# Attention with chosen key chunks, then a squared-ReLU FFN: two heads' scores in 64-row halves, and a mask by DMA

## The chip, the cores and the metric

The kernel runs on one core of a Trainium2 chip. The metric is device time in microseconds, from one launch to the next result; smaller is better. A core has five engines that run side by side, each through its own list of instructions in order: TensorE (PE in the profile; its weight loads are PEld), VectorE (DVE), ScalarE (ACT), GpSimd (POOL) and SyncE (SP). DMA transfers are issued by SP and POOL here and run beside all of them.

## The reference

Four sequences of 768 positions, eight heads of 64, in float32. Keys are cut into 24 chunks of 32. For every query an upper bound of its score with each chunk is made from the chunk's smallest and largest key values; the six best causal chunks are kept, and causal softmax attention runs over those chunks alone. Its output goes through an FFN of 512 to 2048 to 512 with a squared ReLU.

```python
k_min = np.min(k_chunks, axis=3)
k_max = np.max(k_chunks, axis=3)
ub = np.sum(np.maximum(q[:, :, :, None, :] * k_min[:, :, None, :, :],
                       q[:, :, :, None, :] * k_max[:, :, None, :, :]), axis=-1)
ub = np.where(causal, ub, -1000000000.0)
top_chunks = np.argsort(ub, axis=-1)[..., -top_k:]
scores = scale * np.matmul(q, k.transpose(0, 1, 3, 2))
sel = (j_chunk == top_chunks[..., None]).any(axis=-2)
mask = sel & (pos[:, None] >= pos[None, :])
...
return (h * h @ w_out).astype(np.float32)     # h = relu(x @ w_in)
```

## The kernel before

Everything is in bfloat16 with float32 sums. A **tile** is 128 positions, so a sequence has six. The first tile of each sequence sees at most four chunks, so nothing has to be chosen there: `first_attention` (line 556) does plain causal attention for it, and the four first tiles together are one FFN of 512 rows. The other five tiles (640 rows) of each sequence are handled by **pairs** of heads: p = 0 to 15, four pairs a sequence, so pairs 8 to 15 are the last two sequences.

For each pair `stage_a` (line 622) makes the selection. Keys and queries are turned so that the head dimension lies on partitions (by PE for sequences 0 and 1, by DMA transposes on SP for 2 and 3). DVE takes minima and maxima of 32 keys at a time (`kr`, line 690, two passes over 768 columns), splits the queries into a positive and a negative part (`qp`, `qm`, line 706), PE multiplies them (`ub`, lines 656 and 658), DVE adds the causal mask of chunks (line 715), takes the eight best of each row (MAX8, line 664), and compares with the sixth (`selb`, line 720). The comparison is turned (`sT`), and copied into the operands of the scores.

Those operands have 88 rows for one head: 64 of the head and 24 for the chunks. The extra rows of the keys hold -32768 in their own chunk, those of the queries hold 1 for every chunk that was not chosen, so that one matmul gives scores with the unchosen chunks pushed far down. `kqs` and `qss` are the two operands, in four sets, and each head's rows are copied there (`copy`, lines 289 and 291).

`stage_b` (line 759) takes a pair's two heads one after the other. Each head has 20 tiles of scores (key tile by query tile) in five **banks** of four tiles or 512 columns (the list BANKS). For each bank: scores on PE (line 775), exp on ACT (line 797), the diagonal tiles made causal by POOL (line 755) or DVE (line 752), then the product with the values on PE (line 786). `normalise` (lines 604 and 606) divides by the sum.

`ffn` (line 816) turns x (`turn`: by PE for the first tiles and sequences 0 and 3, by DMA for 1 and 2), multiplies with w_in (`up`, line 859), takes ReLU on ACT or DVE (lines 866, 868), squares on DVE (line 877), and multiplies with w_out (`down`, line 890). FFN work of one sequence lies between the attention of the next on PE.

The order of all this is made when the program is built: each operation is given to a `Plan` (line 78) with its engines, costs and a due time, and `order` (line 116) places, again and again, the operation that is due first among those that can start soonest. So each engine's list is fixed in the built program. Where PE would have nothing to do in the first 30 us, `write` (line 203) fills in dummy matmuls (`keep_warm`, line 532, tile `wt`). POOL issues all loads of inputs and weights in a given order with eight outstanding at most; SP issues four first loads, all DMA transposes and the outputs.

Of the kernel before, what the change touches and what calls it, by code (L numbers as in the profile page):

```python
# [9 lines left out]
F32 = mybir.dt.float32  # L10
# [67 lines left out]
class Plan:  # L78
# [13 lines left out]
    NEVER = 1e9  # L92

    def __init__(self, slots, keep_warm, wait):
        self.wait = wait
# [20 lines left out]
    def order(self):  # L116
# [13 lines left out]
        while ready:  # L130
            found = []
            for op in ready:
                if op.packets and not op.turns and op is not self.loads[len(landed)]:
                    continue
                at = 0.0
                new = {}
                for t in op.tiles:
                    if not t.held:
                        new[t.tag] = new.get(t.tag, 0) + 1
                for tag, n in new.items():  # L140
                    at = max(at, sorted(slots[tag])[n - 1][0]
                             if n <= len(slots[tag]) else self.NEVER)
                if at == self.NEVER:
                    continue
                if op.packets and not op.turns and len(landed) >= 8:
                    at = max(at, landed[-8].end)
                for engine, cost in op.where.items():
                    st = max(at, free[engine])
                    for n in op.needs:
                        same = n.engine == engine and not n.packets  # L150
                        lag = (0.0 if engine == "PE" else self.BUSY) if same                             else self.HAND_OVER[n.engine]
                        st = max(st, n.end + lag)
                    for t in op.tiles:
                        if t.psum:
                            for e, end in t.last.items():
                                if e != engine and "PE" not in (e, engine):
                                    st = max(st, end + self.HAND_OVER[e])
                    found.append((st, op, engine, cost))
            assert found, "nothing can start"
            first = min(found, key=lambda f: (f[0], f[1].number))  # L160
            st, op, engine, cost = min(
                (f for f in found if f[2] == first[2] and f[0] <= first[0] + self.wait),
                key=lambda f: (round(f[1].due, 6), f[0], f[1].number))
            ready.remove(op)
# [22 lines left out]
            for n in waiting.get(op, ()):  # L187
                count[n] -= 1
                if not count[n]:
                    ready.append(n)  # L190
            done.append(op)
        assert len(done) == len(self.ops), "operations left"
# [10 lines left out]
    def write(self):  # L203
        idle = 0.0
        for op in self.order():
            if op.engine == "PE":
                free, *bank = self.spare(op.start - 1e-6)
                room = op.start - max(idle, free + self.EARLY)
                if idle and op.start < self.FILL and room >= self.LEAST:
                    self.keep_warm(bank, int((room - self.SPARED) / 0.1092))  # L210
                idle = op.end
            for t in op.tiles:
                if t.tile is None:
                    t.tile = t.make(t.slot)
            op.fn(op.engine)


@with_exitstack
def kernel(
# [51 lines left out]
    psav = ctx.enter_context(tc.tile_pool(name="psav", bufs=1, space=PSUM))  # L271
    psf = ctx.enter_context(tc.tile_pool(name="psf", bufs=1, space=PSUM))

    plan = Plan({"tp": 1, "ps": 3, "av": 2, "ff": 2, "e": 6, "h2": NFI + 6, "ht": 3,
                 "ob": 3, "kq": 6, "nt": 6,
                 "vn": B - 1, "x": 2, "xT": 2,
                 "kr": 2, "qp": 2, "qm": 2, "ubm": 2, "m8": 2, "rc": 2}, lambda *a: keep_warm(*a), P["wait"])
# [709 lines left out]
```

## Time and profile before

| | before |
|---|---|
| median of 3 runs | 263.65 us (263.57 to 263.76) |
| span of the profiled execution | 262.1 us |
| PE busy | 254.6 us, 2435 matmuls |
| DVE busy | 192.2 us |
| ACT busy | 180.2 us |
| POOL busy | 109.4 us |
| DMA | 26.12 MB, 103733 packets |

The profiled execution is known by its span, from its first to its last instruction; its own time with what lies around the span was not taken apart, so the span is set against the median of the runs. In the rows shown further on, a group has a line of the kernel, an engine, an operation, the tiles written and read, a count, then busy us and the mean ns of one, and last the idle time of the engine just before. In rows by time the first two numbers are the start and the length in us. PE busy is counted up to modelled ends, and matmuls overlap, so starts say more than lengths.

### The profile page before, as it was taken

Reading aid. Unit: us, or ns where it says so; the run is one execution under the profiler, and the core shown is the slowest. Engines: PE = TensorE matmul, PEld = TensorE weight load, DVE = VectorE, ACT = ScalarE, POOL = GpSimd, SP = SyncE. Lnnn points to the kernel's source line nnn. Section 1 sums busy time; section 2 is a strip of 40 time slices with the busy share of each in tenths; the row PEclk is TensorE's granted clock in tenths of the full one; section 3 lists DMA queues with packets and bytes.
Section 4 is the critical chain, followed back from the end, with each engine's and each line's share of the span. In section 5 each row is a group of like instructions: output and inputs, shape, how many; then the busy total and the mean of one; then the engine's idle time right before and its main releaser. Section 6 shows DMA issues by size and latency. Waiting matters only on the chain.

```text
span 262.1 us, 6645 instructions
## 1 busy us (share of the span) xinstructions
PE 254.6 (97%) x2435; PEld 168.2 (64%) x2457; DVE 192.2 (73%) x677; ACT 180.2 (69%) x369; POOL 109.4 (42%) x196
## 2 busy tenths in 40 slices
PE   8899999999999999999999999999999999999995
PEld 4678765756687666656786656657767576565443
DVE  5399999968999999999999995886778531254000
ACT  1589798856599888986799847768889351377112
POOL 8997999978416729993121011411103000000000
PEclk9999999999999999999999999999999999999999
DMA  8999999999982999999571011163000011200222
GB/s 134 168 176 187 143 186 166 185 155 195 185 119 46 115 129 175 145 153 134 102 147 57 0 56 43 59 120 94 0 3 0 3 40 40 84 1 0 83 80 80
DMA packets 103733, 26.12 MB, mean 100 GB/s; under 512 B 96332, under 2 KB 100708, under 8 KB 103700
## 3 DMA queue, kind: packets, MB, share of 16 engines
q0 software_dynamic: 75168, 13.33, 65.9%
q1 hardware_dynamic: 28532, 12.36, 22.2%
q8 instruction: 19, 0.31, 0.5%
q14 instruction: 14, 0.11, 0.1%
HBM read 27.26 MB, written 6.29 MB: 128 GB/s over the span
## 4 chain that ended last, share of the span: by engine, by line
PE 89%; ACT 3%; DMA 3%; DVE 2%; issue 1%; SPq 1%; POOL 0%; ACTq 0%; POOLq 0%
PE py L890 31%; PE ph L859 31%; PE ps L775 13%; PE av L786 7%; DMA raw<-in_q_dram 3%; PE wt L537 1%; PE xt L294 1%; ACT qsc L289 1%; ACT ht L866 1%; PE kT L294 1%; SPq L406 1%; PE ub L658 1%; DVE kr L690 1%; PE ub L656 1%; PE qT L294 1%
## 5 line engine op out<-in xcount | busy, mean ns | idle before, releaser
L859 PE MATMUL ph<-xT,w_in_sb 128*128 128x256 bf16 (+2 forms) x592 | 98.0, 304 | 0.5 <-ACT ht L866 0.2
L797 ACT ACTIVATE e<-ps 128x512 bf16<-128x512 f32 x160 | 86.6, 604 | 10.8 <-PE ps L775 6.3
L890 PE MATMUL py<-w_out_sb,h 128*128 128x512 bf16 (+2 forms) x378 | 88.2, 370 | 1.2
L755 POOL TENSOR_SCALAR_AFFINE_SELECT e<-e 128x128 bf16<-128x128 bf16 (+1 forms) x102 | 34.8, 353 | 88.4 <-ACT e L797 79.7
L859 PEld LDWEIGHTS <-w_in_sb 128*128 128x128 bf16 x592 | 55.4, 97 | 24.5 <-issue 1.8
L866 ACT ACTIVATE ht<-ph 128x256 bf16<-128x256 f32 (+2 forms) x122 | 54.9, 455 | 17.2 <-PE ph L859 13.5
L877 DVE TENSOR_TENSOR h<-ht 128x256 bf16<-128x256 bf16 (+2 forms) x148 | 47.4, 330 | 19.9 <-ACT ht L866 13.1
L890 PEld LDWEIGHTS <-h 128*128 128x128 bf16 x400 | 36.5, 98 | 33.1
L775 PE MATMUL ps<-qsc,kqc 88*128 88x128 bf16 (+1 forms) x320 | 54.4, 272 | 0.0
L289 ACT COPY ob<-py 128x512 f32<-128x512 f32 (+2 forms) x22 | 12.5, 568 | 37.3 <-PE py L890 37.2
L786 PEld LDWEIGHTS <-e 128*128 128x128 bf16 x640 | 31.8, 97 | 7.9 <-POOL e L755 0.9
L775 PEld LDWEIGHTS <-kqc 88*128 88x128 bf16 x320 | 27.0, 98 | 11.9 <-issue 0.2
L786 PE MATMUL av<-vn,e 128*128 128x65 bf16 x480 | 32.0, 193 | 0.2 <-POOL e L755 0.2
L606 DVE TENSOR_TENSOR x<-av,rc 128x320 bf16<-128x320 f32 (+1 forms) x40 | 18.6, 470 | 0.3
L690 DVE TENSOR_REDUCE kr<-kT 128x24 bf16<-128x768 bf16 x16 | 14.8, 948 | 1.4 <-PE kT L294 1.4
L664 DVE MAX8 m<-ubm 128x8 f32<-128x24 f32 x160 | 15.6, 169 | 0.0
L690 DVE TENSOR_REDUCE kr<-kt 128x24 bf16<-128x768 bf16 x16 | 14.9, 944 | 0.0
L868 DVE TENSOR_SCALAR ht<-ph 128x256 bf16<-128x256 f32 (+2 forms) x26 | 12.2, 471 | 3.7 <-PE ph L859 3.6
L289 ACT COPY qsc<-sT 24x384 bf16<-24x384 bf16 (+1 forms) x32 | 14.1, 440 | 0.8
L786 PE MATMUL av<-v,e 128*128 128x65 bf16 x160 | 14.0, 193 | 0.0
L454 POOL DMA_DIRECT2D vn<-in_v_dram x15 | 13.3, 901 | 0.5 <-issue 0.5
L537 PE MATMUL wt<-warm 128*128 128x256 bf16 x73 | 11.5, 301 | 1.1 <-DVE warm L358 1.1
(84 smaller groups left out, 251.3 us busy)
## 6 DMA issues: line engine op xcount, KB each, us to landing
out_dram<-ob SPq DMA_DIRECT2D x23, 256.0 KB, 2.3
w_in_sb<-in_moe_w_in_dram POOLq DMA_DIRECT2D x4, 512.0 KB, 7.6
w_out_sb<-in_moe_w_out_dram POOLq DMA_DIRECT2D x4, 512.0 KB, 8.3
vn<-in_v_dram POOLq DMA_DIRECT2D x15, 128.0 KB, 5.7
nt<-in_k_dram POOLq DMA_DIRECT2D x10, 128.0 KB, 5.4
nt<-in_q_dram POOLq DMA_DIRECT2D x10, 128.0 KB, 5.7
kn<-in_k_dram POOLq DMA_DIRECT2D x8, 80.0 KB, 6.7
qn<-in_q_dram POOLq DMA_DIRECT2D x8, 80.0 KB, 6.7
```

Of the source, the lines that this page charges most:

```text
L289: nc.scalar.copy(dst, src)
L606: return plan.op({"DVE": 0.06 + 0.00108 * D * n}, due, lambda _: nc.vector.tensor_mul(x(), av[:, :, 0:D], rc[:, 0:n].unsqueeze(2).to_broad ...
L664: nc.vector.max(out=m8[:, i, hh], in_=ubm[:, i, hh])
L690: nc.vector.tensor_reduce(kr[:, mm].rearrange("d (t c) -> d t c", c=128 // CH) if b >= BY_DMA else kr[:, mm], part(kT).rearrange("d t (c j ...
L755: nc.gpsimd.affine_select(out=e, in_=e, compare_op=ALU.is_ge, fill=0.0, base=0, channel_multiplier=-1, pattern=[[0, n], [1, 128]])
L775: nc.tensor.matmul(ps[:, 128 * c:128 * (c + nt)], lhsT=kqs[:, s, hh, 128 * j:128 * (j + 1)], rhs=qss[:, s, hh, 128 * (t0 - 1):128 * (t0 - ...
L786: nc.tensor.matmul(av[:, t - 1], lhsT=e[:, 128 * c:128 * (c + 1)], rhs=value_tile(b, h, j), start=(i == 0 and c == 0), stop=(i == len(BANK ...
L797: nc.scalar.activation(e.tile, ps.tile, ACT.Exp, scale=scale), [sc], [ps, e])
L859: nc.tensor.matmul(ph.tile, lhsT=w_in_sb[:, ki, 128 * f:128 * (f + 1)], rhs=xT[:, c0 // 128:c1 // 128, ki], start=(ki == 0), stop=(ki == N ...
L866: nc.scalar.activation(ht.tile, ph.tile, ACT.Relu)
L877: {"DVE": 0.067 + w / 1920}, at[0] + P["h2"], lambda _: nc.vector.tensor_mul(h2[f][:, c0:c1], ht.tile, ht.tile), [op], [ht, h2[f]])))
L890: nc.tensor.matmul(py.tile, lhsT=h2[f][:, 128 * t:128 * (t + 1)], rhs=w_out_sb[:, f, c0:c1], start=(f == 0), stop=(f == NFI - 1))
```

## The change

It has five parts, which stand in one diff.

1. **Pairs 8 to 15.** Their score operands are no longer the copies of 88 rows. The two heads' keys and queries are read where the DMA transposes put them, one head in partitions 0 to 63, the other in 64 to 127, and the matmuls of the two heads stand next to each other (`stage_b_rows`). They come in three groups a pair: four banks, four, two. The first key tile comes from a new tile `k1t`, which `first_transposes` fills.
2. **The mask.** Without the extra rows the choice is applied after exp. The turned selection of a pair is written to DRAM four times (`rowm`), then read back by six transfers that repeat each chunk's row over its 32 keys (`keep`, two buffers of 20 tiles x 2 heads). POOL makes the diagonal tiles of the mask causal, and DVE multiplies each bank's e with it: 80 multiplies, in the place of selects on the diagonals alone.
3. **Passes of DVE.** Minima and maxima of sequences 2 and 3 by a tree of halving passes over two pairs at once; the causal mask of chunks is added to the diagonal chunks alone, MAX8 reads only the chunks that can be seen, and copies and negative parts may go to ACT. Squares may go to ACT.
4. **Smaller ones.** The last sequence's x is turned by DMA; the first attention of sequences 2 and 3 has its diagonal cut after exp rather than by matmuls ahead of the scores (`preset`); the score operands have two sets, not four; `early` holds the first queries and later the first x.
5. **The order.** `Plan.order` takes each engine's list from ORDER, written out by number; costs and due times no longer decide it. Dummy matmuls stand only behind the first ten, which now come just ahead of pair 0's scores.

Counts in the two built programs:

| | before | after |
|---|---|---|
| PE: matmuls in all | 2459 | 2377 |
| PE: dummies (`wt`) | 73 | 15 |
| PE: transposes of x | 56 | 36 |
| PE: presets of 512 columns | 8 | 4 |
| DVE: mask multiplies | 0 | 80 |
| DVE: squares / ReLUs | 148 / 26 | 89 / 58 |
| ACT: squares / ReLUs | 0 / 122 | 59 / 90 |
| POOL: selects on e / on the mask | 102 / 0 | 46 / 40 |
| SP: plain transfers of the mask | 0 | 80 |
| SP: DMA transposes of x | 10 | 15 |

```diff
@@ Plan.order
-        ready = [op for op in self.ops if not count[op]]
+        at = {e: 0 for e in self.given}
+        while len(done) < len(self.ops):
             found = []
-            for op in ready:
+            for engine, line in self.given.items():
+                op = self.ops[line[at[engine]]]
...
+ORDER = {e: [int(i) for i in text.split()] for e, text in {
+    "PE": """
+        129 145 127 125 130 141 277 143 170 282 132 146 138 172 288 174 148 157 185 155 341
...
@@ kernel
-    VW = 80
+    VW = 72
     NSET = 4
+    KSET = 2
+    RP = 8
+    ROWS = RP // NP
+    COPIES = 4
...
-        s = plan.op({"PE": 0.44}, due - 5, preset, [made["ahead"], made["ident"], q0.op if b > 1 else None], ps)
+        s = None
+        if b < 2:
+            s = plan.op({"PE": 0.44}, due - 5, preset, [made["ahead"], made["ident"]], ps)
...
+            if b > 1:
+                e = plan.op({"DVE": 0.33, "POOL": 0.62}, due + 0.4, lambda en, hh=hh:
+                            causal(en, es[hh].tile, NP), [e, made["tri"]], [es[hh]])
...
+    def spread(p, t, sT, rowm, due):
+        m = keep[p]
+        held_back = kept_before[-1:]
+        out = [plan.op({"SP": 0.5}, due + 0.1 * i, lambda _, i=i: nc.sync.dma_start(
+            out=rowm.tile[:, i].rearrange("c t hh q -> c t (hh q)"),
+            in_=sT.tile[0:NC * NS].rearrange("x hh q -> x (hh q)")),
+            [t], [sT, rowm], packets=160, turns=True, late=0.7)
+            for i in range(COPIES)]
+        kept = {}
+        for j in range(NT):
+            n = NT - max(1, j)
+            kept[j] = plan.op({"SP": 0.5}, due + 1 + 0.1 * j, lambda _, j=j, n=n: nc.sync.dma_start(
+                out=m[:, ROW[j]:ROW[j] + n].rearrange("k t hh q -> k (t hh q)"),
+                in_=rowm.tile[4 * j:4 * j + 4, :, max(1, j) - 1:NS].rearrange(
+                    "a r t hh q -> (a r) (t hh q)").unsqueeze(1).to_broadcast(
+                        [4 * COPIES, CH // COPIES, 256 * n])),
+                out + held_back, [rowm, m], packets=200 * n, turns=True, late=0.7)
...
+    HELD = [(0, 1), (2, 3), (4,)]
...
+            def scores(_, banks=banks, pss_=pss_):
+                for i in banks:
+                    c = 0
+                    for j in range(NT):
...
+                        for hh in range(2):
+                            rows = slice(D * hh, D * hh + D)
+                            nc.tensor.matmul(
+                                pss_[i, hh][:, 128 * c:128 * (c + len(ts))],
+                                lhsT=keys(rows, j),
+                                rhs=queries(rows, ts[0], ts[-1] + 1),
+                                start=True, stop=True)
...
+                    mu = plan.op({"DVE": 0.334}, due + P["vm"], lambda _, e=e, i=i, hh=hh:
+                                 nc.vector.tensor_mul(
+                                     e.tile.rearrange("k (t q) -> k t q", q=128),
+                                     e.tile.rearrange("k (t q) -> k t q", q=128), m[:, 4 * i:4 * i + 4, hh]),
+                                 [ex] + prepared[p, "keep"], [e, m])
...
@@ the last FFN
-            0 < b < B - 1, HALVES * NP * (b + 1) + P["due"][b], P["rate"][b],
+            0 < b, HALVES * NP * (b + 1) + P["due"][b], P["rate"][b],
```

More of the change, by code (lines that the diff above doesn't have):

```diff
@@ L139, in order @@
                         new[t.tag] = new.get(t.tag, 0) + 1
+                    elif t.psum:
+                        for e, end in t.last.items():
+                            if e != engine and "PE" not in (e, engine):
+                                st = max(st, end + self.HAND_OVER[e])
+                if any(n > len(slots[tag]) for tag, n in new.items()):
+                    continue
                 for tag, n in new.items():
-                    at = max(at, sorted(slots[tag])[n - 1][0]
-                             if n <= len(slots[tag]) else self.NEVER)
@@ L143, in order @@
-                if at == self.NEVER:
-                    continue
+                    st = max(st, sorted(slots[tag])[n - 1][0])
                 if op.packets and not op.turns and len(landed) >= 8:
[L146 to L158, printed above, removed]
@@ L159, in order @@
-            assert found, "nothing can start"
[L160 to L164, printed above, removed]
+                    st = max(st, landed[-8].end)
+                for n in op.needs:
+                    same = n.engine == engine and not n.packets
+                    lag = (0.0 if engine == "PE" else self.BUSY) if same \
+                        else self.HAND_OVER[n.engine]
+                    st = max(st, n.end + lag)
@@ L678, in stage_a @@
         if b >= BY_DMA:
+            before = []
             got = list(loaded["k", b])
```

460 lines of the change are left out of this document (334 added, 126 removed), and 91 rows, old and new, of the table ORDER.

## The prediction

> **What bounds the kernel now.** I read the page's busy times and its chain of waits first, then a table of four stretches of the run, then the order of instructions on single engines where a price was needed.
>
> ```profile
> span 262.1 us, 6645 instructions
> PE 254.6 (97%) x2435; PEld 168.2 (64%) x2457; DVE 192.2 (73%) x677; ACT 180.2 (69%) x369; POOL 109.4 (42%) x196
> PE 89%; ACT 3%; DMA 3%; DVE 2%; issue 1%; SPq 1%; POOL 0%; ACTq 0%; POOLq 0%
> ```
>
> TensorE is busy 97% of the span and carries 89% of the chain that ended last. The stretches (ends chosen at the first up-projection matmul, the first scores of pair 8, the last scores) tell where the rest is. Columns: PE, weight loads, DVE, ACT, POOL, then clock, DMA share, GB/s.
>
> ```profile
> 0.00:21.83 21.83, 19.30 (x206) 13.90 (x207) 14.44 (x62) 12.77 (x21) 20.64 (x31) 1.00 1.63 164
> 21.83:115.00 93.17, 92.28 (x1001) 63.10 (x1010) 87.50 (x307) 76.79 (x158) 69.30 (x113) 1.00 1.67 152
> 115.00:204.00 89.00, 88.23 (x895) 59.82 (x901) 75.09 (x264) 69.50 (x148) 19.47 (x54) 1.00 0.39 65
> 204.00:262.10 58.10, 54.79 (x341) 31.41 (x344) 15.18 (x46) 21.09 (x46) 0.00 (x0) 1.00 0.12 46
> ```
>
> From 21.83 on PE is busy 99% of every stretch until the last output copy. So a us of PE work taken out there is a us of time, and a us on any other engine is worth nothing until it makes PE wait. The first 21.83 us are different: PE is filled with dummy matmuls, and the start-up chain (loads, casts, selection of pair 0) sets the length.
>
> ```profile
> L537 PE MATMUL wt<-warm 128*128 128x256 bf16 x73 | 11.5, 301 | 1.1 <-DVE warm L358 1.1
> L859 PE MATMUL ph<-xT,w_in_sb 128*128 128x256 bf16 x288 | 38.7, 272 | 0.5 <-ACT ht L866 0.2
> ```
>
> **The scores (pairs 8 to 15).** What counts on PE is the distance between starts, not the duration of one. First a run of scores as they are, then the only place where the kernel already puts two heads into 64-row halves, the first attention (L573, 64 rows each, heads alternating).
>
> ```profile
> 109.03 0.82 PE L775 MATMUL ps<-qsc,kqc 88*128 88x128 bf16 x6
> 109.69 0.23 PE L786 MATMUL av<-v,e 128*128 128x65 bf16 x2
> ...
> 19.27 0.34 PE L294 MATMUL sT<-ident,selb 128*128 128x128 bf16 x3
> 19.55 0.40 PE L573 MATMUL ps<-t,t 64*128 64x128 bf16 x8
> 19.88 0.40 PE L294 MATMUL xt<-ident,x 128*128 128x128 bf16 x4
> 20.11 1.15 PE L537 MATMUL wt<-warm 128*128 128x256 bf16 x9
> ```
>
> Six score matmuls are three banks of 512 columns: 109.69 - 109.03 = 0.66, so 0.22 a bank and 10 x 0.22 = 2.20 us a pair. Four full-height transposes of 128 columns take 20.11 - 19.88 = 0.23, or 0.057 each. Eight half-height matmuls of the same width take 19.88 - 19.55 = 0.33. One after another they would need 8 x 0.057 = 0.46; fully side by side 0.23. They do run side by side, and the missing 0.10 is a price for going back to full height. The three transposes before them take 0.28 where 3 x 0.057 = 0.17 would do: another 0.11 on the way in. So a group of paired scores costs about 0.21 beside its columns. The new code makes three groups a pair of heads (four, four and two banks): 5 x 0.22 + 3 x 0.21 = 1.73 us. Saved: 2.20 - 1.73 = 0.47, times 8 pairs = 3.8 us. Ends: 1.1 x 8 = 8.8 if the switches were free; -5.0 (a loss) if wide halves did not overlap and the switches still cost 0.63 a pair. I take 3.8, the row's own rate.
>
> The Trainium skill, "TensorEngine Tiling (Array Packing)", says under "Key Properties" that a change of tiling mode drains the array, and under "Theoretical Speedup" that 64 rows give up to twice the rate. By the second alone the sum would have 8.8 for 3.8; the row above agrees with the first, at about 0.1 us a change.
>
> **Other PE work.** The last sequence's x goes to a DMA transpose: 5 x 0.23 = 1.15 us of PE off the dense stretch. The causal presets of sequences 2 and 3 go (four matmuls of 512 columns, about 1 us), but they lie before 21.83 among dummies: 0, at most 1.0. The 73 dummies become 15; they fill waits, so they count 0 by themselves.
>
> **DVE, ACT, POOL.** Per pair the late copies into the score operands go, and the key minima and maxima become a tree of halving passes; in their place each of the ten banks gets a mask multiply, 80 in all, nearest to the 512-wide square.
>
> ```profile
> L690 DVE TENSOR_REDUCE kr<-kt 128x24 bf16<-128x768 bf16 x16 | 14.9, 944 | 0.0
> L291 DVE COPY qsc<-qt 64x640 bf16<-64x640 bf16 x16 | 7.6, 475 | 0.3
> L291 DVE COPY kqc<-kt 64x768 bf16<-64x768 bf16 x16 | 6.5, 409 | 0.2
> L877 DVE TENSOR_TENSOR h<-ht 128x512 bf16<-128x512 bf16 x12 | 5.0, 437 | 0.3 <-ACT ht L866 0.2
> L877 DVE TENSOR_TENSOR h<-ht 128x256 bf16<-128x256 bf16 (+2 forms) x148 | 47.4, 330 | 19.9 <-ACT ht L866 13.1
> L868 DVE TENSOR_SCALAR ht<-ph 128x256 bf16<-128x256 f32 (+2 forms) x26 | 12.2, 471 | 3.7 <-PE ph L859 3.6
> L866 ACT ACTIVATE ht<-ph 128x256 bf16<-128x256 f32 (+2 forms) x122 | 54.9, 455 | 17.2 <-PE ph L859 13.5
> L606 DVE TENSOR_TENSOR x<-av,rc 128x320 bf16<-128x320 f32 x32 | 15.4, 484 | 0.3
> L604 DVE RECIPROCAL rc<-av 128x5 f32<-128x5 f32 x32 | 5.9, 188 | 2.0 <-PE av L786 1.7
> 17.63 0.95 DVE L664 MAX8 m<-ubm 128x8 f32<-128x24 f32 x10
> ```
>
> Ten MAX8 of mean 169 ns fill 0.95 us, so a pass holds DVE some 0.08 us less than its mean. Out: 29.0 - 48 x 0.08 = 25.2 us. In: 80 x (0.437 - 0.08) = 28.6, and 8 trees of some 1,490 columns each, at that rate about 1.2 us each, 9.6. Squares (59 to ACT) and ReLUs (32 back from ACT) nearly cancel: 59 x 0.33 against 32 x 0.47, -4. Net about +9 us for DVE in a stretch where it idles 89.0 - 75.1 = 13.9. ACT gains some (59 - 32) x 0.455 = 12 us over the run, with 19.5 idle in that stretch. POOL swaps its selects on e for 40 on the mask, at 19.5 busy of 89. All cost 0 while PE has other matmuls in hand; uncovered, the worst is the DVE's fill: about 90%, where its in-order queue passes waits on.
>
> **The mask and SP's queue.** SP gets 80 more plain transfers (per pair four to DRAM, six back) and five more transposes, all in one queue.
>
> ```profile
> L903 SPq DMA_DIRECT2D out_dram<-ob x25: 332/333/571, 57.1 to 259.4; - x25
> DMA to landing us min/median/max: 1.6/2.3/5.7
> ...
> L396 SPq DMA_TRANSPOSE sT<-selb x8: 1177/1198/1220, 104.8 to 178.2; - x8
> DMA to landing us min/median/max: 2.3/2.3/5.6
> ...
> L396 SPq DMA_TRANSPOSE xT<-x x10: 1189/1260/1647, 118.9 to 176.8; - x10
> DMA to landing us min/median/max: 2.5/2.5/4.3
> L755 POOL TENSOR_SCALAR_AFFINE_SELECT e<-e 128x256 bf16<-128x256 bf16 x24 | 10.1, 421 | 12.1 <-ACT e L797 11.8 <-DVE h L877 0.2
> ```
>
> Issue: 80 x 0.33 to 0.57 = 27 to 46 us of an SP that is free most of 89; DMA's share there is 0.39 of 10. A mask buffer (two exist) comes free at the last multiply of pair p - 2, and pair p's first multiply needs all six transfers and the select behind the last. That turn takes 6 x 0.33 + 2.3 + 0.42 = 4.7 us at least and 6 x 0.57 + 5.7 + 0.42 = 9.5 at most. Eight pairs in 115 to 204 have 11 us each, so one pair's own time, less some 2 us in which neighbours overlap, covers up to 9. Taken: 0, near the median landing; at most 0.5 to 1 us a pair if the end is met.
>
> Tail: after the last value product PE still has 44 down matmuls. Nineteen of them stand here:
>
> ```profile
> 150.25 4.48 PE L890 MATMUL py<-w_out_sb,h 128*128 128x512 bf16 x19
> 154.57 0.53 PE L786 MATMUL av<-vn,e 128*128 128x65 bf16 x12
> ```
>
> At 4 in 0.86 (0.216 each, some records missing here) that is 9.5 us of cover. The x of the last sequence needs two normalisations (each 0.19 + 0.48), two transposes on SP (2 x 1.26) and a landing (2.5 to 4.3): 6.4 to 8.2. It fits. Two output writes behind the five transposes wait about 6.3 us, inside the same cover; cost 0, up to 1 if the third output buffer blocks.
>
> **The start.** The first up matmul needs the first slice of w_in.
>
> ```profile
> 13.38 0.79 POOL L468 DMA_DIRECT2D w_in_sb<-in_moe_w_in_dram  x1
> 20.42 1.71 POOL L461 DMA_DIRECT2D kn<-in_k_dram  x2 [0.45 <-DMA w_in_sb<-in_moe_w_in_dram]
> 11.51 0.22 PE L294 MATMUL kT<-ident,k 128*128 128x128 bf16 x1
> 3.23 1.91 PE L564 MATMUL ps<-ahead,ident 128*128 128x512 bf16 x4
> 4.94 0.63 PE L294 MATMUL T<-ident,k 128*128 128x128 bf16 x4
> 9.42 0.39 PE L294 MATMUL T<-ident,q 128*128 128x128 bf16 x4
> ```
>
> It landed at 20.42, 1.4 us ahead of its first use. The new POOL order issues it one load later (about 0.9 us), so that it holds the dense part to 21.3 or later however fast the rest is. The loads of pair 0's keys move to the front of POOL (an issue of about 1.0 goes from ahead of them), so its chain, which began on PE at 11.51, may start 1 to 2 us sooner. I take 0: bounds -2.0 (chain sooner and w_in early) and +1.5.
>
> **The sum.** Against the profiled execution: span 262.1 - 3.8 - 1.15 = 257.15. The median of the runs stands 263.65 - 262.1 = 1.55 above the span; the same is kept: 258.7. Faster by 1.9%.
>
> **Rivals.**
> - The mask comes late (slower). Everything above 9 us in the turn of a mask buffer is paid at each of pairs 10 to 15, with DVE's queue stopped and PE behind it. It decides from about 9.8 us on (0.8 x 6 = 4.9 eats the gain). At 11 us: 258.7 + 2 x 6 = 270.7; a second landing in the median (2.3, DRAM written before it is read) paid once per pair would make 258.7 + 6 x 2.3 = 272.5. For it: ten transfers through one queue, two buffers. Against: DMA nearly idle there, PE has FFN work of the sequence before. 0.14.
> - No side-by-side at 256 to 512 columns (slower): 263.65 + 5.0 - 1.15 = 267.5. Against: L573's narrow halves do overlap, and nothing in the trace ties that to width. 0.03.
> - PE cold at the start. Presets at 3.23 took 1.91 for four and transposes at 4.94 0.63 for four, against 0.39 at 9.42: early matmuls ran at half speed, with PE filled from 1.13 on. In the new order the fill stands only ahead of the first scores. From that fill on it was still slow after 3.8 us (4.94) and at full rate after 8.3 (9.42). If the array is slow again when the dense part begins, half of such a time is lost: 1.9 to 4.1, so 260.6 to 262.8. The Trainium skill, "TensorE: Matmul & The Clock Gate", "Part 1: The HAM clock gate (the “warmup” mystery)", says full clock comes after a window of about 3.4 us of sustained work and is lost after an idle one; this trace shows the start, not the loss. 0.13.
> - A shorter start: pair 0's chain 2 us sooner and w_in not later: 256.7. For it: DVE constants shrink and the two presets ahead of the first selection transpose go. Against: w_in. 0.17.
> - No change: gain eaten by small waits, within 0.5: 0.03.
>
> **The numbers.** The forecast itself (257.5 to 260) has 0.50; shorter start 0.17, cold start 0.13: together faster 0.80. Within 0.2% (about what a measurement of this kernel tells from no change) 0.03; slower 0.14 + 0.03 = 0.17. The range goes from 255.5 (start 2 us shorter plus part of the 1.0 of presets) to 264.5, which leaves out most of the slower cases (0.13) and little below (0.06). The likeliest one's own range is 257 to 260.5.
>
> **What would show it.** Paired scores: about 1.7 us of PE per pair, three groups, with some 0.1 us before and behind each. First up matmul between 20 and 23 us, and granted clock full from it on. PE busy 99% from there to the last output. Waits of the mask multiplies: on ACT (exp) if right, on POOL's select or on DMA of the mask if the turn is late. The last sequence's first up matmul without a wait for its transposes. The prediction fails if PE shows idle pieces behind the value products of pairs 10 to 15, or if the dense part begins after 23 us.

## The result and the profile after

The changed kernel takes 288.5 us (median of 4 runs, 287.2 to 289.2) against 263.7 before: a ratio of 1.092 (95% interval 1.087 to 1.096). The forecast was 258.7, so it missed by 30 us and had the sign wrong. Two of the versions further on had one execution each that was over 1.5% above the fastest of its version; their medians are those of the other executions. The page of the changed kernel answers the three lines shown of the kernel before:

```profile
span 287.5 us, 6578 instructions
PE 255.4 (89%) x2353; PEld 159.7 (56%) x2375; DVE 192.4 (67%) x698; ACT 188.7 (66%) x398; POOL 107.2 (37%) x181
PE 56%; SPq 11%; DVE 9%; DMA 9%; POOL 5%; issue 5%; ACT 4%; POOLq 0%; ACTq 0%; DVEq 0%
```

PE is no longer dense: it carries 56% of the chain that ended last where it carried 89%, and SP's queue, which had 1%, carries 11%. A table of windows says where (columns as in the prediction):

```profile
0.00:26.00 26.00, 16.74 (x139) 11.66 (x140) 15.34 (x58) 12.69 (x21) 21.07 (x32) 1.00 1.67 149
26.00:120.00 94.00, 90.99 (x959) 61.22 (x965) 81.30 (x297) 83.77 (x173) 68.49 (x107) 1.00 1.77 144
120.00:220.00 100.00, 83.71 (x812) 50.16 (x821) 68.75 (x271) 63.97 (x141) 16.02 (x39) 0.95 0.69 178
```

Three places lose time. From 120 to 220, where the mask is made, PE stands still for 16.3 us, and the granted clock is no longer full. The start has 9.3 us without PE work, against 2.5 in the first 26 us of the kernel before. Between them 3.0 are lost, against 0.9 before.

**The stretch of the mask.** These are the rows of the mask's transfers, SP's DMA transposes and the outputs, from the answers for single tiles of the changed kernel (issue time in ns: minimum, median, maximum; then first and last start):

```profile
L1001 SPq DMA_DIRECT2D keep<-rowm x48: 514/597/2041, 132.4 to 215.2; - x48
...
L993 SPq DMA_DIRECT2D rowm<-sT x32: 742/785/1532, 125.6 to 201.2; - x32
...
L502 SPq DMA_TRANSPOSE sT<-selb x8: 1167/1228/1952, 115.9 to 181.0; - x8
...
L502 SPq DMA_TRANSPOSE xT<-x x15: 1210/1265/2230, 128.8 to 246.3; - x15
...
L1278 SPq DMA_DIRECT2D out_dram<-ob x25: 332/449/587, 80.7 to 284.5; - x25
```

The forecast took an issue for 0.33 to 0.57, from the output rows. A write to DRAM holds SP's queue for 0.785 and a read back for 0.597. I added up all of SP's rows that start from 119.83 to 213.90: 32 writes 27.0, 48 reads 33.1, 19 transposes 25.3, 11 outputs 5.4, together 90.8 of 95.9 us. A row also holds the short gaps between its issues; the issues alone come to some 87 us, and in the same stretch of the kernel before to 30. Of the other 9 us hardly any is a wait for the mask's own transfers: the waits view of SP in this stretch has 0.2 us for them. SP's queue is full, and what stands in it comes late: mask, outputs, transposes.

Two examples from the timeline of the changed kernel; the brackets hold the idle time ahead and what ended it:

```profile
139.86 1.12 POOL L666 TENSOR_SCALAR_AFFINE_SELECT keep<-keep 128x256 bf16<-128x256 bf16 x3 [2.10 <-DMA keep<-rowm]
140.65 0.95 DVE L1150 TENSOR_TENSOR e<-e,keep 128x512 bf16<-128x512 bf16 x2 [1.99 <-DMA keep<-rowm]
...
142.53 0.59 ACT L395 COPY ob<-py 128x512 f32<-128x512 f32 x1 [5.24 <-DMA out_dram<-ob]
143.16 1.01 PE L1224 MATMUL ph<-xT,w_in_sb 128*128 128x256 bf16 x4 [3.85 <-ACT ob L395]
...
214.03 1.12 POOL L666 TENSOR_SCALAR_AFFINE_SELECT keep<-keep 128x256 bf16<-128x256 bf16 x3 [12.38 <-DMA keep<-rowm]
214.83 0.60 DVE L1150 TENSOR_TENSOR e<-e,keep 128x512 bf16<-128x512 bf16 x1 [4.72 <-POOL keep L666]
...
216.62 2.32 PE L1224 MATMUL ph<-xT,w_in_sb 128*128 128x384 bf16 x8 [4.35 <-DVE ht L1233]
```

In the first, PE's wait is not for the mask at all. The output copied by 129.46 was issued only at 137.91, behind the mask's issues, so ACT had no output buffer for 5.24 us, and PE behind ACT waited 3.85. In the run without the mask's transfers below, the issue of the same output starts at 128.29, and its buffer causes no such wait.

The second is the mask's own chain, and the longest wait of PE in the run: the mask lands late, POOL's select behind it holds up a multiply at the head of DVE's queue, a ReLU stands behind that, and PE waits 4.35 for it.

After the first hole four up matmuls take 1.01, where four of the same shape take 0.60 in a row of the fill-first run below. The window says that the array lost its clock there:

```profile
140.00:150.00 10.00, 6.84 (x51) 4.61 (x51) 5.70 (x17) 5.49 (x13) 0.98 (x3) 0.66 0.52 104
```

**The start.** PE's rows of the changed kernel, in time order:

```profile
7.40 0.61 PE L687 MATMUL ps<-t,t 64*128 64x128 bf16 x8 [0.84 <-DVE ubmask L445]
...
18.21 0.63 PE L400 MATMUL T<-ident,k 128*128 128x128 bf16 x4
...
23.30 2.31 PE L637 MATMUL wt<-warm 128*128 128x256 bf16 x10 [1.18 <-DVE early L725]
25.40 0.64 PE L1049 MATMUL ps<-qsc,kqc 88*128 88x256 bf16 x2
25.83 1.06 PE L1224 MATMUL ph<-xT,w_in_sb 128*128 128x256 bf16 x4
...
27.78 1.79 PE L1224 MATMUL ph<-xT,w_in_sb 128*128 128x256 bf16 x8
...
30.70 0.60 PE L1224 MATMUL ph<-xT,w_in_sb 128*128 128x256 bf16 x4
```

The first up matmul starts at 25.83, 4.0 us later than before. The matmuls up to there run at half rate (0.63 for four transposes, 0.39 in the quoted row of before), and the ten dummies, which wait for a buffer that DVE frees, are now in the path: 2.3 us at half rate, directly ahead of the dense part. The half rate also goes on into the dense part: four up matmuls take 1.06 at 25.83 and 0.60 only at 30.70. So the start costs more than the 4.0 us.

### The profile page after: what moved, and what is told of

Its sections match the earlier page's. It is cut to its first block, busy times and chain, and to the rows that moved or that the text cites. A ratio compares the mean times of both kernels' runs of the same rounds, so it can differ in the third digit from the quotient of the medians.

```text
span 287.5 us, 6578 instructions
## 1 busy us (share of the span) xinstructions
PE 255.4 (89%) x2353; PEld 159.7 (56%) x2375; DVE 192.4 (67%) x698; ACT 188.7 (66%) x398; POOL 107.2 (37%) x181
## 2 busy tenths in 40 slices
DMA packets 115444, 38.55 MB, mean 134 GB/s; under 512 B 98084, under 2 KB 109384, under 8 KB 115412
## 4 chain that ended last, share of the span: by engine, by line
PE 56%; SPq 11%; DVE 9%; DMA 9%; POOL 5%; issue 5%; ACT 4%; POOLq 0%; ACTq 0%; DVEq 0%
PE ph L1224 23%; PE py L1264 18%; SPq L1001 5%; DMA keep<-rowm 5%; PE ps L1049 4%; SPq L993 4%; PE av L1060 3%; DMA v<-in_v_dram 2%; SPq L502 2%; PE av L1157 2%; DMA out_dram<-ob 2%; PE ps L1132 2%; POOL vn L554 1%; PE wt L637 1%; POOL e L666 1%
## 5 line engine op out<-in xcount | busy, mean ns | idle before, releaser
L1231 ACT ACTIVATE ht<-ph 128x256 bf16<-128x256 f32 (+2 forms) x90 | 40.3, 454 | 21.1 <-PE ph L1224 16.9
L1147 ACT ACTIVATE e<-ps 128x512 bf16<-128x512 f32 x80 | 44.1, 601 | 14.3 <-PE ps L1132 12.9
L666 POOL TENSOR_SCALAR_AFFINE_SELECT keep<-keep 128x256 bf16<-128x256 bf16 x40 | 16.3, 433 | 81.3 <-DMA keep<-rowm 70.5
L1150 DVE TENSOR_TENSOR e<-e,keep 128x512 bf16<-128x512 bf16 x80 | 31.5, 425 | 19.5 <-POOL keep L666 10.0
L1247 DVE TENSOR_TENSOR h<-ht 128x384 bf16<-128x384 bf16 (+2 forms) x89 | 29.0, 337 | 18.0 <-ACT ht L1231 17.4
L1233 DVE TENSOR_SCALAR ht<-ph 128x256 bf16<-128x256 f32 (+2 forms) x58 | 28.5, 492 | 15.2 <-PE ph L1224 11.5
L1245 ACT ACTIVATE h<-ht 128x256 bf16<-128x256 bf16 (+2 forms) x59 | 27.1, 472 | 10.5 <-DVE ht L1233 10.2
L1049 PE MATMUL ps<-qsc,kqc 88*128 88x128 bf16 (+2 forms) x160 | 27.3, 277 | 0.1
L666 POOL TENSOR_SCALAR_AFFINE_SELECT e<-e 128x128 bf16<-128x128 bf16 (+2 forms) x46 | 16.5, 371 | 26.3 <-ACT e L1071 22.2
L1060 PE MATMUL av<-vn,e 128*128 128x65 bf16 x240 | 15.6, 193 | 1.4 <-DVE e L663 0.9
L723 DVE RECIPROCAL rc<-av 128x5 f32<-128x5 f32 (+1 forms) x40 | 7.1, 186 | 12.9 <-PE av L1157 5.6
L725 DVE TENSOR_TENSOR x<-av,rc 128x320 bf16<-128x320 f32 x32 | 15.0, 476 | 0.1
```

The lines of the kernel that those rows point to most:

```text
L666: nc.gpsimd.affine_select(out=e, in_=e, compare_op=ALU.is_ge, fill=0.0, base=0, channel_multiplier=-1, pattern=[[0, n], [1, 128]])
L1049: nc.tensor.matmul(ps[:, 128 * c:128 * (c + nt)], lhsT=kqs[:, ks, hh, 128 * j:128 * (j + 1)], rhs=qss[:, ks, hh, 128 * (t0 - 1):128 * (t0 ...
L1060: nc.tensor.matmul(av[:, t - 1], lhsT=e[:, 128 * c:128 * (c + 1)], rhs=value_tile(b, h, j), start=(i == 0 and c == 0), stop=(i == len(BANK ...
L1147: nc.scalar.activation(e.tile, ps.tile, ACT.Exp, scale=scale), [sc], [ps, e])
L1150: nc.vector.tensor_mul(e.tile.rearrange("k (t q) -> k t q", q=128), e.tile.rearrange("k (t q) -> k t q", q=128), m[:, 4 * i:4 * i + 4, hh]),
L1231: nc.scalar.activation(ht.tile, ph.tile, ACT.Relu)
```

## The experiments

Each edit is made on the changed kernel unless said otherwise. Ratios are to the kernel before as it ran beside each version (medians of 264.0 to 264.4 us).

**Leave the mask's transfers out.** The 32 writes, the 48 reads and the selects on the mask are dropped; the multiplies stay and take a constant triangle.

```diff
-                                     e.tile.rearrange("k (t q) -> k t q", q=128), m[:, 4 * i:4 * i + 4, hh]),
+                                     e.tile.rearrange("k (t q) -> k t q", q=128), tri.unsqueeze(1).to_broadcast([128, 4, 128])),
```

> Leaves out the mask of pairs 8 to 15: the 80 transfers that write and read it and POOL's 40 selects on it are gone, and the 80 DVE multiplies stay but take a constant triangle; PE's matmuls and every engine's order stay. Theory M (SP's queue is full with the mask between 125 and 216 us: 32 x 0.79 + 48 x 0.60 = 54 us of issue beside some 34 us of transposes and outputs): about 15 us of PE's idle time between 120 and 220 us go, so 288.5 falls to 270 to 275. Theory O (the written-out order does not fit the real durations, whatever the mask does): most of that idle time stays, 282 to 288. Theory S (the start alone): no change, 288.

Measured: 268.8 us (two runs), ratio 1.016 (1.010 to 1.022), 19.7 less than the changed kernel. Its window row:

```profile
120.00:220.00 100.00, 98.13 (x993) 59.50 (x1004) 79.61 (x304) 75.94 (x167) 1.30 (x2) 1.00 0.25 52
```

PE is dense again at full clock. So 19.7 of the 24.8 us lost hang on the transfers.

**Run the transfers, but wait for none.** The same constant in the multiplies; all transfers and selects run.

> As the changed kernel with all 80 transfers and POOL's selects on the mask, but the DVE multiplies take a constant triangle and so wait for none of it (the mask of pairs 8 to 15 is left out of the result). If the loss of M comes from multiplies that wait for the mask, it falls to 270 to 275 as without the transfers. If it comes from what else stands in SP's queue (outputs, turned x, turned selections) behind the mask's issues, it stays above 280. A split shows the two shares.

Measured: 281.6 us (two runs), ratio 1.064 (1.057 to 1.071): only 6.9 less. The stretch stays broken though no multiply waits for the mask. Its window row, then PE's two longest waits in it:

```profile
120.00:220.00 100.00, 88.50 (x879) 54.14 (x888) 73.80 (x278) 68.36 (x152) 21.01 (x42) 0.95 0.71 176
```

```profile
141.32 1.01 PE L1224 MATMUL ph<-xT,w_in_sb 128*128 128x256 bf16 x4 [2.71 <-ACT ob L395]
...
193.13 1.04 PE L1224 MATMUL ph<-xT,w_in_sb 128*128 128x256 bf16 x4 [5.79 <-DMA xT<-x]
```

So of the 19.7, 6.9 are waits of the multiplies, and 12.8 come from what the transfers do to everything else. The rows show to what: an output buffer that came free late, and a transpose of x that landed late.

**Let POOL issue the writes to DRAM.** This takes 27 us of issues off SP and leaves every transfer as it was.

```diff
-        out = [plan.op({"SP": 0.5}, due + 0.1 * i, lambda _, i=i: nc.sync.dma_start(
+        out = [plan.op({"SP": 0.5}, due + 0.1 * i, lambda _, i=i: nc.gpsimd.dma_start(
```

> The 32 writes of the turned selection to DRAM are issued by POOL at the same places of the plan, so SP loses 32 x 0.79 = 25 of about 88 us of issue between 125 and 216 us; transfers, sizes and engines' orders stay. If SP's issue time is the bound there: 8 to 13 us off, 275 to 281. If the round trip through DRAM is (write, receipt, read), it moves under 3 us, and gets worse where POOL's own descriptor work of about 0.9 each is later than SP's.

Measured: 270.8 us, ratio 1.029 (1.024 to 1.033): 17.7 less, with the same bytes moved (38.55 MB in both). The waits view, then the rows of the two kinds of transfer:

```profile
POOL keep L666 <- DMA keep<-rowm: 41.4, 14, 10.3
```

```profile
L1001 SPq DMA_DIRECT2D keep<-rowm x48: 515/597/1641, 127.2 to 198.7; - x48
L993 POOL DMA_DIRECT2D rowm<-sT x32: 627/627/720, 121.5 to 184.3; - x32
```

POOL's wait for the mask was 70.5 us in the changed kernel (16 times, 12.9 at the longest). SP's issues now fill some 59 of the 95.9 us. So most of the 19.7 hangs on what stands in SP's queue, not on the bytes, which are the same here. The issue times fit this; that the writes now also go through another queue of transfers was not tested apart. Some of the gain may be chance: the edit leaves the start alone, yet in the profiled execution the first up matmul comes at 24.28, 1.5 us sooner than in that of the changed kernel.

**One copy in DRAM instead of four.** 8 writes for 32; the six reads take all rows from the one copy.

```diff
-                in_=rowm.tile[4 * j:4 * j + 4, :, max(1, j) - 1:NS].rearrange(
-                    "a r t hh q -> (a r) (t hh q)").unsqueeze(1).to_broadcast(
-                        [4 * COPIES, CH // COPIES, 256 * n])),
+                in_=rowm.tile[4 * j:4 * j + 4, 0, max(1, j) - 1:NS].rearrange(
+                    "a t hh q -> a (t hh q)").unsqueeze(1).to_broadcast(
+                        [4, CH, 256 * n])),
```

> The turned selection of each pair is written to DRAM once, not four times (8 transfers for 32), and the six read transfers of a pair repeat its rows 32 times, not 8. Theory M: 24 x 0.79 = 19 us of SP's issue time go, the queue falls from about 88 to 69 us of 90, and the time by 8 to 14 us, 274 to 281. Theory O: under 3 us. If four readers of one row are slow in DRAM, the landings get longer than now and the gain is smaller.

Measured: 327.9 us, ratio 1.238 (1.231 to 1.245): 39 us slower, though SP issues 24 transfers fewer. Waits of this run:

```profile
POOL keep L666 <- DMA keep<-rowm: 123.1, 23, 15.7
...
DVE e L1150 <- DMA keep<-rowm: 27.2, 5, 10.0
```

The slowest dimension of the source went from 16 to 4. Counted over the packets of 2560 bytes, which in this stretch only these reads have, some 3.6 ran at once, against 9.5 in the changed kernel. One packet was not slower (116 ns in the mean, 144 there), so four readers of one row, the expectation's other reason, are not it. The Trainium skill, "DMA: Bandwidth & Descriptors", under "Why a DMA increments its semaphore by 16 and not by 1", says that a transfer is spread over the largest number of engines, at most 16, that divides the slowest dimension of both sides. By that rule it is 4 here and 16 in the changed kernel; the trace agrees with the 4. The four copies, which looked like waste, are what spreads the reads.

**The fill first.** The dummies and the memset of their source go to the front of PE's and DVE's lists, and dummies may stand before them too, as before the change.

```diff
-        129 145 127 125 130 141 277 143 170 282 132 146 138 172 288 174 148 157 185 155 341
-        177 294 152 187 159 124 299 189 320 307 167 198 192 162 182 315 303 346 332 195 328
+        124 129 145 127 125 130 141 277 143 170 282 132 146 138 172 288 174 148 157 185 155 341
+        177 294 152 187 159 299 189 320 307 167 198 192 162 182 315 303 346 332 195 328
...
-                if warmed and op.start < self.FILL and room >= self.LEAST:
+                if idle and op.start < self.FILL and room >= self.LEAST:
```

> The ten first dummies and the memset that they read go to the front of PE's and DVE's lists, and idle time after them is filled again in the first 30 us, as in the kernel before; all else stays. Theory S (dummies at half clock stand in the path: 2.3 us from 23.3, and PE runs at half speed up to about 25 us): first up matmul at 21 to 23 instead of 25.8 and 3 to 5 us off, 283.5 to 285.5. Theory M alone, or O: within 1 us of 288.5, since slack later is eaten by the mask's queue.

Measured: 281.7 us, ratio 1.063 (1.057 to 1.069), 6.8 less. PE's rows of this run:

```profile
14.79 0.40 PE L687 MATMUL ps<-t,k1t 64*128 64x128 bf16 x8
...
22.62 0.60 PE L1224 MATMUL ph<-xT,w_in_sb 128*128 128x256 bf16 x4
```

The eight half-height matmuls take 0.40 where they took 0.61, and the first up matmul comes 3.2 us sooner, at full rate. Since the changed kernel then runs on at half rate, its matmuls of the same work lie 4.6 us behind those of this run from 34 to 137 us. So the start is worth 4.6; the other 2.2 us lie later, where the mask comes, and were not taken apart.

**Both together.** First without the mask's transfers and with the fill first:

> Both causes taken out at once: no mask transfers and selects (the mask of pairs 8 to 15 is left out of the result, its multiplies take a constant triangle), and the dummies first. If the two losses are separate, the gains add: 288.5 - 19.7 - 6.8 = 262.0, and the kernel is about where the old one is, since PE's own saving of about 5 us is still partly lost between 26 and 140 us. If nothing but the two went wrong with the forecast, it comes to 258 to 260. If the start is paid back later (O), 266 to 269.

Measured: 265.2 us, ratio 1.005 (1.003 to 1.008). Then with POOL issuing the writes and the fill first:

> The writes by POOL and the dummies first, all results kept. If both gains hold and add: 268 to 275. If either is eaten by the other, no better than 280. Below 263 it would beat the kernel before.

Measured: 269.5 us, ratio 1.022 (1.019 to 1.025). The gains do not add up: the fill brings 6.8 alone, 3.6 on top of the first edit and 1.3 on top of the other, in whose profiled execution the start had already come sooner.

**Share the reads with POOL too.** On top of the last one, POOL also issues the reads of three of the six key tiles.

```diff
-            kept[j] = plan.op({"SP": 0.5}, due + 1 + 0.1 * j, lambda _, j=j, n=n: nc.sync.dma_start(
+            kept[j] = plan.op({"SP": 0.5}, due + 1 + 0.1 * j, lambda _, j=j, n=n: (nc.gpsimd if j > 2 else nc.sync).dma_start(
```

> The changed kernel with the fill first, the mask's 32 writes to DRAM issued by POOL, and of its 48 reads the last three key tiles of each pair (24) by POOL too. Theory Q (the time that the queue's issues take is all that is left beside the start): SP then issues 24 x 0.60 + 34 = 48 us of the 90 and POOL about 56 x 0.63 = 35 us more; waits of POOL for the mask go under 20 us, the waits of the mask multiplies under 3 us, and the time comes within 2 us of the run without the transfers (265.2): 265 to 267. Rival W (the way through DRAM itself is too long: write, landing, read, landing, whoever issues it): POOL's waits for the mask stay near 40 us and the time near that of the run with only the writes by POOL, 269 to 270. Rival P (POOL's own queue now holds up its selects): above 270, with waits of the multiplies for POOL's select above 10 us.

Measured: 268.1 us, ratio 1.017 (1.010 to 1.025). Its three executions go from 267.4 to 271.1, so the 1.4 us under the last run are not clear of the scatter. POOL's waits for the mask did fall to 19.8 (as theory Q had it), but the time is above that theory's 265 to 267; rival W, which had the waits near 40, does not hold either. One turn of a mask buffer is left that is late, in the timeline of the slowest of the three:

```profile
196.36 0.40 POOL L666 TENSOR_SCALAR_AFFINE_SELECT keep<-keep 128x256 bf16<-128x256 bf16 x1 [6.95 <-DMA keep<-rowm]
...
197.84 0.61 DVE L1150 TENSOR_TENSOR e<-e,keep 128x512 bf16<-128x512 bf16 x1 [3.10 <-POOL keep L666]
...
199.77 0.48 PE L1224 MATMUL ph<-xT,w_in_sb 128*128 128x384 bf16 x2 [2.88 <-DVE ht L1233]
```

This is again the chain of the first rival: mask, POOL's select, a multiply at the head of DVE's queue, a ReLU behind it, PE. It costs 2.9 us in one place. With the writes on POOL, 4.3 us are left between the mask's transfers and none (269.5 against 265.2); how they divide between the way through DRAM, POOL's selects and the issues that stay was not shown.

**Another order.** The changed operations, but ordered by due times as in the kernel before.

```diff
-            for engine, line in self.given.items():
-                op = self.ops[line[at[engine]]]
+            for op in ready:
...
+            first = min(found, key=lambda f: (f[0], f[1].number))
```

> The changed operations, but each engine's list is made by the planner of the kernel before from its costs and due times instead of the written-out lists (its dummies first, as there). Theory O (the lists are the fault): below 275. Theory M: the mask's 80 transfers still stand in SP's queue, and nothing better than 280 comes out; the start, which has its fill ahead again, may give 3 to 6 us of it.

Measured: 285.5 us, ratio 1.082 (1.079 to 1.086): 3.0 less. That alone looked as if the order hardly mattered. With the writes on POOL and costs nearer to the trace (0.62 for a read on SP, where it has 0.597; 0.9 for a write on POOL, where it has 0.627):

> The changed operations in the order that due times make, as one run before, but with the mask's writes on POOL and the costs of these issues as the trace has them (0.62 for an issue of SP, 0.9 for one of POOL, where 0.5 stood). Theory Q: the queue is what costs, so the gain over the due-time run (285.5) is that of the same move under the written-out order (17 us): 267 to 270; the written-out order is worth no more than 3 us either way. Rival O (the written-out order was made around another arrangement and is at fault): under 265.

Measured: 280.5 us, ratio 1.058 (1.052 to 1.065). Neither expectation holds: the move was worth 17.7 under the written-out lists and is worth 5 here, where the new costs changed the lists as well. POOL still waits long for the mask (waits view of this run):

```profile
POOL keep L674 <- DMA keep<-rowm: 48.8, 17, 18.2
```

And without the mask's transfers and selects:

> The changed operations without the mask's transfers and selects (multiplies by a constant triangle, the mask is not applied), in the order that due times make instead of the written-out lists. Rival: the written-out lists leave PE the small waits (it stood at 268.8 without the transfers, first up matmul at 25.8; the due-time order brought that to 20.9 before): 259 to 262. Theory: the operations themselves leave them (DVE's passes for the keys stand ahead of what PE waits for in either order), the start gives about 3: 265 to 267. Above 268: the written-out order is the better one.

Measured: 278.4 us, ratio 1.052 (1.046 to 1.059), against 268.8 under the written-out lists. So the written-out order is the better one by 10 us, although the first up matmul comes later in it (25.20 for 20.80). With SP's queue full that did not show. Both orders are still planned with the mask's operations in them.

**No multiplies.** On the run of 265.2 us, the 80 multiplies go too.

```diff
-                    mu = plan.op({"DVE": 0.334}, due + P["vm"], lambda _, e=e, i=i, hh=hh:
-                                 nc.vector.tensor_mul(
+                    mu = plan.op({"DVE": 0.334}, due + P["vm"], lambda _: None,
```

> As the run without the mask's transfers and with the fill first (265.2), and the 80 multiplies are left out too, so e goes from exp to the values as it is (the mask is not applied). Step d of the forecast said that DVE's fill costs nothing. If that holds, 31 us less of DVE from 119 us on change little: 264 to 265.2. If DVE's fill is what keeps that run 6.5 above the forecast: 259 to 261, with the waits of PE for DVE gone. What lies between says how much of it the multiplies hold.

Measured: 265.7 us, ratio 1.006 (1.004 to 1.008). DVE is busy 27 us less (164.7 against 191.7), and nothing is gained. From 26 to 140 us, mostly ahead of the first multiply, PE works as long with them as without; from 140 to 220 it is busy throughout in both. The row of the kernel before, then that of the run with them, then without:

```profile
26.00:140.00 114.00, 113.01 (x1205) 77.22 (x1216) 107.39 (x378) 92.33 (x192) 73.97 (x125) 1.00 1.51 146
```

```profile
26.00:140.00 114.00, 109.47 (x1163) 71.63 (x1162) 101.24 (x400) 97.01 (x205) 66.96 (x105) 1.00 1.50 139
```

```profile
26.00:140.00 114.00, 109.47 (x1163) 71.59 (x1162) 97.91 (x390) 97.01 (x205) 66.98 (x105) 1.00 1.51 139
```

**One part alone, on the kernel before.** Only the last sequence's x is turned by DMA.

```diff
-            0 < b < B - 1, HALVES * NP * (b + 1) + P["due"][b], P["rate"][b],
+            0 < b, HALVES * NP * (b + 1) + P["due"][b], P["rate"][b],
```

> The kernel before, with one part of the change alone: the last sequence's x is turned by DMA transposes. The forecast's term: 5 x 0.23 = 1.15 us of PE off the dense tail, the landing covered by down matmuls of the sequence before: 262.5 to 263, ratio 0.995 to 0.997. Rival: the landing is not covered, since outputs and five transposes of 1.2 us each stand in one queue of SP: PE's first up matmuls of the last sequence wait 1 us or more, ratio 1.000 to 1.015.

Measured: 262.75 us, ratio 0.995 (0.992 to 0.998). This is the one version that comes out below the kernel before, by 0.5%. PE goes from the down matmuls to the last up matmuls without a wait:

```profile
204.84 8.80 PE L890 MATMUL py<-w_out_sb,h 128*128 128x512 bf16 x40
213.47 5.40 PE L859 MATMUL ph<-xT,w_in_sb 128*128 128x256 bf16 x48
218.72 3.62 PE L890 MATMUL py<-w_out_sb,h 128*128 128x512 bf16 x16
```

## Why the prediction was wrong

**What bounds the kernel: right.** In every run the lost time stood on PE, as holes or as matmuls at half rate behind them.

**The scores: right.** Three groups of one pair in the changed kernel, with the rows around them:

```profile
180.60 0.40 PE L1132 MATMUL ps<-qt,kt 64*128 64x128 bf16 x6
180.93 0.29 PE L1157 MATMUL av<-vn,e 128*128 128x65 bf16 x4
...
183.50 0.45 PE L1132 MATMUL ps<-qt,k1t 64*128 64x512 bf16 x4
183.78 0.33 PE L1132 MATMUL ps<-qt,kt 64*128 64x384 bf16 x2
184.04 2.76 PE L1264 MATMUL py<-w_out_sb,h 128*128 128x512 bf16 x12
186.73 0.61 PE L1132 MATMUL ps<-qt,kt 64*128 64x256 bf16 x8
187.27 2.76 PE L1264 MATMUL py<-w_out_sb,h 128*128 128x512 bf16 x11
```

From the first start of a group to the next row: 0.33 for two banks, and 0.54 twice for four. That is 1.41, with the way out in it. The way in I took from all starts of the run of 265.2 us: some 0.096 a group. Together 1.70 a pair, where the forecast said 1.73. A change of tiling does cost about 0.1. The Trainium skill, "TensorEngine Tiling (Array Packing)", under "Theoretical Speedup", gives up to 2× for 64 rows; by that alone a pair would have taken 1.10 (an estimate).

**The last x: right.** Forecast -1.15; alone it brought a ratio of 0.995, some 1.2 us with an interval of 0.4 to 2.1. That the two agree to a tenth is luck: the profiled executions differ by 1.9 us, and 0.95 of that lies at the start, where the first up matmul came at 20.88 for 21.83.

**DVE and ACT: right for the multiplies.** A multiply took 425 ns where 437 was forecast, and all 80 together cost nothing. (The step's own sum makes DVE 94% full, not about 90%.) This row of the changed kernel also shows what their queue waited for:

```profile
L1150 DVE TENSOR_TENSOR e<-e,keep 128x512 bf16<-128x512 bf16 x80 | 31.5, 425 | 19.5 <-POOL keep L666 10.0 <-DMA keep<-rowm 3.9 <-ACT e L1147 2.9
```

**The mask and SP's queue: here it failed.** The step said "Issue: 80 x 0.33 to 0.57 = 27 to 46 us of an SP that is free most of 89" and took 0. Three things were wrong in it. The issue was sized by the row of the outputs, which have another shape; writes and reads of the mask took 0.785 and 0.597, some 60 us together by the sum above. SP's own transposes and outputs, 31 us, were not added to it, though rows of 1.2 us for the transposes stood quoted right above; they were only the reason for "most" in "free most of 89". 60 and 31 make 91, more than the 89. And the cost was looked for in the mask's turn alone, where 6.9 of 19.7 were found; the 12.8 were paid by outputs and transposes behind the mask in the same queue. The step also read the DMA column as "0.39 of 10"; it is the busy share of the engines, so 39%, and the rival's "DMA nearly idle there" had less behind it than it seemed. The first rival, the late mask (270.7 to 272.5, at 0.14), had the sign and one of the two mechanisms, priced by landings.

**The start: here it failed too.** It was taken as 0, with bounds of -2.0 and +1.5; the first up matmul came 4.0 later, and the matmuls behind it lost some 1.4 more at half rate (4.6 less 3.2, against the fill-first run). The step counted the dummies, 73 to 15, as nothing "by themselves". But the remaining ones were moved into the path, and the gaps that the others had filled left PE at half rate. The rival of a cold start (0.13) had the mechanism, priced at 1.9 to 4.1 for the dense part; that part lost about 1.4, and the later beginning was in no rival. It was held to be one case or the other with the late mask; both came.

**The tail: right.** In the changed kernel the five transposes of the last x were issued by 246.3, and the first long run of up matmuls, at 250.16, waited for nothing.

**What stays open.** Without the mask's transfers and with the fill first, the kernel takes 265.2, still 6.5 above the forecast. In spans, 263.4 against 257.15. The start has 0.7 of it (first up matmul at 22.49 for 21.83). Holes from 26 to 140 have 3.5 (4.5 idle against 1.0 in the rows above). Among them PE waits for DVE's keys (two waits, 1.5 us together) and for e (0.9). They are neither the multiplies' nor cured by the due-time order, which has 7.0 us idle in the same stretch. Whether the new passes for the keys cause them wasn't tried. About 2 us more were not found. They may belong to the same waits: idle time counts from modelled ends, so it is shorter than a wait. At 105.97 of the run of 265.2 us it gives 0.49, where PE's next matmul starts 0.66 later than at the usual distance. This is not shown for the others.

## What to carry to other kernels

Before work is moved to a queue that looks idle, add up all that the queue issues in that stretch, with the issue time of each kind and shape, and price kinds that the trace lacks well above the cheapest one it shows. Then ask who else stands in that queue: here outputs and transposes behind the mask cost twice what the mask's own lateness did. Fill work at the start isn't free to remove or to move: it keeps the matmuls at full rate and must not stand ahead of the first dense work.

## What the runs showed of the hardware that was not expected

- In the median an issue on SP took 0.449 us for an output, 0.597 for a read of the mask, 0.785 for a write of 120 rows to DRAM, and about 1.2 for a DMA transpose; POOL issued the same write to DRAM in 0.627.
- Reading with a slowest source dimension of 4 instead of 16 made the kernel 39 us slower, although fewer transfers were issued.
- The array lost its clock in the middle of the run: with a hole of 3.85 us in it, the window from 140 to 150 shows a granted clock of 0.66. The trace before showed slow matmuls at the start alone. The Trainium skill, "TensorE: Matmul & The Clock Gate", "Part 1: The HAM clock gate (the “warmup” mystery)", says that full clock is lost after an idle window. This trace agrees.
- In the start of the changed kernel the clock column reads 1.00 while the matmuls run at half rate; there their lengths tell it, and the column does not. In the run with the writes on POOL, whose start has the same order, it shows a lower clock (0.83, the first number behind POOL's):

```profile
0.00:26.00 26.00, 17.62 (x147) 11.74 (x148) 15.51 (x58) 13.79 (x24) 21.96 (x34) 0.83 1.78 156
```
